# Two softmaxes' results transposed by DMA in five of eight batches, stores of the middle tiles on another queue, and a new order

## The chip, the cores and the metric

The kernel runs on one core of one Trainium2 chip. A core has a matrix engine (TensorE, PE in the profile; its weight loads have a row of their own, PEld), a vector engine (VectorE, DVE), a scalar engine (ScalarE, ACT), GpSimd (POOL) and a queue engine that only issues transfers (SyncE, SP). They run side by side and wait for each other through semaphores; each carries out its own instructions in the order in which the program lists them. The metric is the device time of one execution in microseconds, lower is better.

## What is computed

Attention through 32 packed queries per head, and then a feed-forward block with a squared ReLU, over 8 batches of 576 tokens, 8 heads of 64:

```
def sm_attn(qq, kk, vv):
    s = scale * np.matmul(qq, kk.transpose(0, 1, 3, 2))
    a = exp(s - max(s));  a = a / sum(a)
    return np.matmul(a, vv)
p_packed = sm_attn(p, k, v)                    # first softmax, over 576 keys
out = sm_attn(q, p_packed, p_packed)           # second softmax, over 32 packed keys
x = out.transpose(0, 2, 1, 3).reshape(4608, 512)
g = np.maximum(x @ w_in, 0.0) ** 2             # w_in 512 x 2048
result = g @ w_out                             # w_out 2048 x 512, float32
```

## The kernel before

All matrix work is in bf16, accumulated in float32 in PSUM. The eight heads of a batch are taken as two groups of four (the index `qd`), so that 4 x 32 packed queries fill 128 rows. For each batch b the steps are:

- **Tk, Tq**: VectorE transposes the loaded k and q in 32 x 32 blocks (lines 391 and 396).
- **S1**: scores of the packed queries on TensorE (405, 407), then maximum, exponential and normalization; the normalized result is the tile `e1n` (422).
- **E**: `s1_tr` turns `e1n` by five 128 x 128 transposes on TensorE (428) into PSUM, and `s1_out` copies that to the tile `e1` in SBUF, on VectorE or ScalarE. Once for each `qd`.
- **PV**: `e1` times v (442), and **XT**: the packed values are copied out, in two forms.
- **M**: the packed values times w_in (469), copied out as `M`. The second attention is thus folded into the first feed-forward product: its output is never formed.
- **S2**, **C**: scores of the 576 queries against the packed keys (490, 508), then maximum, difference, exponential, sum and product; the result is `n2` (543).
- **N**: `s2_trh` turns `n2` by four and by five TensorE transposes (552, 554), and `s2_outh` copies them to the tile `a2`, in two halves.
- **F1**: for each of 16 blocks of 128 hidden columns, `f1_mm` multiplies `M` with `a2` over two groups and two halves of 288 tokens (567), `f1_relu` (605) and `f1_sq` (615) make the squared ReLU in `gT`.
- **F2**: for each of the 36 tiles of 128 tokens, 16 matmuls of `gT` with w_out (623); `f2_out` copies the sum to `o_sb` (three buffers) and stores it by four DMAs of 64 KB on SyncE's queue (632).

Batch 0 is handled in smaller halves (`SOLO`). Inputs are loaded by GpSimd's queue (363 to 375), which issues its last load at 91 us of the profile. `keep_clock` puts matmuls on a tile of zeros (306) into TensorE's queue where the plan sees a gap in the first 70 us.

The order of all this is computed when the kernel is built. `Plan` simulates engines, PSUM banks and buffers: a `Step` has pieces with an engine and a cost, the steps it depends on, and a `lag` after its end (for a transfer). Whenever an engine is free, the ready step with the lowest priority value goes next; the priorities are the level of the step's kind plus an entry in `TABLE` that was found by a search. The instructions are then emitted in the order of the plan's starts, and each engine carries out its part in that order, whatever the true durations are.

Of the kernel before, what the change touches and what calls it, by code (L numbers as in the profile page):

```python
# [14 lines left out]
P = 128  # L15
# [34 lines left out]
class Plan:  # L50
# [179 lines left out]
TABLE = {'o': {'F2.10': 9.46, 'Tk.7': 21.4, 'Tq.7': 33.99, 'S1.7': 1.48, 'E.7': 32.14, 'PV.7': 37.91, 'XT.7': 25.64,  # L230
    'M.7': -16.57, 'S2.7': 25.07, 'C.7': 3.76, 'N.7': -24.34, 'F1.7': 11.4, 'F2.6': 17.88, 'M.5': 28.2, 'F2.11': 4.52,
    'P.0': -15.37, 'P.2': 23.02, 'PV.0': 41.78, 'PV.1': -18.07, 'PV.2': -170.61, 'PV.3': 15.6, 'PV.4': 24.74, 'PV.5':
    50.46, 'PV.6': 36.59, 'F2.28': 22.46, 'Tk.2': -5.46, 'Tq.2': 29.94, 'S1.2': -31.94, 'E.2': -12.36, 'XT.2': -89.86,
    'M.2': 21.02, 'S2.2': -17.52, 'C.2': -43.11, 'N.2': -66.16, 'F1.2': -77.2, 'F2.2': 9.33, 'E.1': -3.03, 'S2.0':
    -23.17, 'S2.1': -77.35, 'S2.3': 25.69, 'S2.4': 2.43, 'S2.5': 19.07, 'S2.6': -43.31, 'F1.4': 22.5, 'X.0': 4.02,
    'I2': -4.34, 'Tq.0': 41.62, 'C.3': 12.43, 'I': -21.13, 'Tk.4': 7.8, 'Tq.4': 73.53, 'S1.4': 6.89, 'E.4': -35.44,
    'XT.4': 13.78, 'M.4': 27.57, 'C.4': -22.86, 'N.4': -40.64, 'Tk.3': -2.54, 'Tq.3': 0.13, 'S1.3': -18.78, 'E.3':
    -37.22, 'XT.3': -50.22, 'M.3': 5.0, 'N.3': -11.14, 'F1.3': -41.33, 'F2.7': 8.19, 'Tq.1': -7.08, 'F2.32': -13.57,
    'C.1': -39.73, 'F2.0': 16.2, 'F2.4': 12.03, 'F2.8': -33.24, 'F2.12': -104.27, 'F2.14': -11.93, 'F2.16': -31.57,
    'F2.18': 50.59, 'F2.20': 10.93, 'F2.22': 58.58, 'F2.24': 12.61, 'F2.26': 28.84, 'F2.30': -32.16, 'F2.34': 11.76,  # L240
    'F2.1': 6.19, 'F2.3': 15.65, 'F2.5': -3.27, 'F2.9': 56.43, 'F2.13': 87.78, 'F2.15': 66.49, 'F2.17': 33.58,
    'F2.19': 23.11, 'F2.21': -9.88, 'F2.23': -16.12, 'F2.25': 1.33, 'F2.27': -3.46, 'F2.29': -57.09, 'F2.31': 10.9,
    'F2.33': 10.56, 'F2.35': 8.17, 'FA.0': -13.56, 'XT.1': 1.11, 'E.0': 7.63, 'Tk.6': 27.02, 'Tq.6': 35.38, 'S1.6':
    -0.9, 'E.6': 21.43, 'XT.6': -24.73, 'M.6': -14.77, 'C.6': -27.6, 'N.6': -21.43, 'F1.6': 9.04, 'N.1': -24.39,
    'F1.0': 11.32, 'F1.1': -44.14, 'F1.5': 16.32, 'XT.0': 18.01, 'XT.5': 3.63, 'Tq.5': 37.3, 'Tk.5': 9.59, 'S1.5':
    -29.87, 'E.5': 38.05, 'C.5': 8.51, 'N.5': -3.11, 'X.1': 22.86, 'N.0': -4.85, 'M.0': 35.02, 'M.1': -66.62, 'Tk.1':
    -11.6, 'S1.1': -31.8, 'S1.0': 10.99, 'Tk.0': -5.05}, 'l': {'M.0': -0.4, 'M.1': -0.6, 'M.2': -4.65, 'M.3': -1.76,
    'M.4': 0.35, 'M.5': -0.84, 'M.6': -1.62, 'M.7': 0.92, 'F2.0': -2.74, 'F2.2': -0.16, 'F2.4': 0.92, 'F2.6': -3.13,
    'F2.8': -2.6, 'F2.10': -1.26, 'F2.12': -1.09, 'F2.14': -0.1, 'F2.16': -1.84, 'F2.18': 2.67, 'F2.20': 3.0, 'F2.22':
    -0.29, 'F2.24': 0.61, 'F2.26': 1.34, 'F2.28': -0.04, 'F2.30': -2.69, 'F2.32': 0.95, 'F2.34': 0.34, 'F2.1': -0.07,  # L250
    'F2.3': -1.89, 'F2.5': -1.27, 'F2.7': -2.34, 'F2.9': 2.49, 'F2.11': 4.97, 'F2.13': 0.8, 'F2.15': -0.27, 'F2.17':
    1.19, 'F2.19': 0.34, 'F2.21': -3.12, 'F2.23': -0.33, 'F2.25': 1.96, 'F2.27': 0.05, 'F2.29': 0.52, 'F2.31': -0.53,
    'F2.33': -0.9, 'F2.35': -1.42, 'E.3': 5.1, 'E.5': 0.76, 'N.6': -0.01, 'E.4': 3.71, 'N.7': 0.63, 'E.0': 0.73,
    'XT.1': -0.94, 'XT.3': -0.28, 'XT.4': -5.82, 'XT.5': -0.78, 'X.1': 1.12, 'N.5': -2.41, 'XT.6': -0.27, 'N.0': 1.97,
    'F1.1': -2.19, 'E.6': 0.46, 'E.2': 0.97, 'N.1': 3.16, 'XT.2': -2.27, 'N.3': -0.26, 'N.2': -0.79, 'E.7': 0.19,
    'XT.7': 1.48, 'XT.0': -1.64, 'N.4': -1.73, 'E.1': 1.06, 'X.0': 0.41}, 'w': 0.17, 'm': 33.05}


def kernel_impl(tc, q, k, v, p, w_in, w_out, out):
# [13 lines left out]
    TOKH = (2 * P, S - 2 * P)  # L273

    with ExitStack() as ctx:
# [102 lines left out]
        class Att:  # L378
# [105 lines left out]
            def s2(self, u):  # L484
                self.ps2 = pair(u)
                for tt in range(4):
                    for qd in range(NQD):
                        c0 = (tt % 2) * 2 * P + qd * P
                        for dh in range(2):
                            nc.tensor.matmul(self.ps2[:, tt // 2, c0:c0 + P], lhsT=self.qT[:, qd, dh, tt * P:(tt + 1) * P],  # L490
                                             rhs=self.pq_of(qd, dh), start=(dh == 0), stop=(dh == 1))
# [64 lines left out]

            def s2_outh(self, x, eng):
                self.tile_of("a2", att, [P, NQD, S], BF16)
                cast(eng, self.a2[:, :, x * 2 * P:x * 2 * P + TOKH[x]], self.pst[x].rearrange("p (q n) -> p q n", q=NQD))

        ph, rr = {}, {}

        def f1_mm(a, fb, u):
            ps = ph[a.b, fb] = pair(u)[:, :, :HALF]
            for qd in range(NQD):
                for c in range(2):
                    nc.tensor.matmul(ps[:, c], lhsT=a.M[:, qd, fb * FB:(fb + 1) * FB],  # L567
                                     rhs=a.a2[:, qd, c * HALF:(c + 1) * HALF],
                                     start=(qd == 0), stop=(qd == NQD - 1))

        def new_r(a, fb):
            rr[a.b, fb] = Att.cols(rpool.tile([P, 2 * TOKH[1]], BF16, name="r"))

# [26 lines left out]
        def f1_relu(a, fb, eng, c0=0, c1=2):  # L600
            if c0 == 0:
                new_r(a, fb)
            dst, src = rr[a.b, fb][:, c0:c1], ph[a.b, fb][:, c0:c1]
            if eng is nc.scalar:
                nc.scalar.activation(dst, src, ACT.Relu)  # L605
            else:
                nc.vector.tensor_scalar_max(dst, src, 0.0)

        def f1_sq(a, fb, eng):
            o = (a.b % 2) * S  # L610
            r = rr[a.b, fb]
            if eng is nc.scalar:
                nc.scalar.activation(Att.cols(gT[:, fb, o:o + S]), r, ACT.Square)
            else:
                eng.tensor_tensor(out=Att.cols(gT[:, fb, o:o + S]), in0=r, in1=r, op=ALU.mult)  # L615
# [10 lines left out]
        def f2_out(t, eng):  # L626
            ob = opool.tile([P, NE], F32, name="o_sb")
            cast(eng, ob, po[t])
            for i in range(4):
                b, j = divmod(t * 4 + i, JT)  # L630
                dst = out[b * S:(b + 1) * S, :].rearrange("(a j) e -> j a e", j=JT)[j]
                nc.sync.dma_start(dst, ob[32 * i:32 * i + 32, :])  # L632
# [37 lines left out]
        def tr_steps(b, nm):  # L670
# [6 lines left out]
            return [Step(f"T{nm}.{b}.{qd}", [[[("DVE", 1.36, lambda qd=qd: (T[b].tr_k if nm == "k" else T[b].tr_q)(qd))]]],  # L677
                         [f"L{nm}.{b}.{qd}"] + old + gate(b, 0 if nm == "k" else 2), (), [("kqb", 0, f"L{nm}.{b}.{qd}")]) for qd in QDS]

        def s1_steps(b):  # L680
# [8 lines left out]
            def two(qd):  # L689
                nm = f"E.{b}.{qd}"  # L690
                return Step(nm, [[[("PE", 0.28, lambda: T[b].s1_tr(qd, U[nm]))]],
# [4 lines left out]
        def pv_steps(b):  # L696
            nm = f"PV.{b}.0"
            return [Step(nm, [[[("PE", 0.43, lambda: T[b].pv(0, U[nm]))]]],
                         [f"E.{b}.0", f"Lv.{b}.0", f"Lv.{b}.1", "I2" if b else "I"], banks=AB),
                    Step(f"PV.{b}.1", [[[("PE", 0.43, lambda: T[b].pv(1, U[nm]))]]],  # L700
# [40 lines left out]
        def s2_steps(b):  # L741
# [20 lines left out]
            if b in SOLO:  # L762
# [4 lines left out]
                                                     pre, banks=AB + OB, free=[(2, None)]), nstep(1, [f"S2.{b}.1", f"S2.{b}.2"], AB + OB)]  # L767
            return [Step(nm, [a] + front(3, 1024), pre, banks=HB, free=[(2, None)]),
                    Step(nr, [r] + front(2, 128), pre, banks=AB, free=[(2, None)]),
                    Step(f"C.{b}", chain(4, 1152), [nm, nr])] + [nstep(x, [f"C.{b}"], AB) for x in range(2)]  # L770
# [11 lines left out]
        def f1_steps(b):  # L782
# [3 lines left out]
            for fb in range(NFB):  # L786
                nm = f"F1.{b}.{fb}"
                if b in SPLIT:
                    relu = [[("ACT", 0.42, lambda fb=fb, x=x: f1_relu(T[b], fb, A, x, x + 1)),
                             ("DVE", 0.45, lambda fb=fb, x=x: f1_relu(T[b], fb, V, x, x + 1))] for x in range(2)]  # L790
                else:
                    relu = [[("ACT", 0.66, lambda fb=fb: f1_relu(T[b], fb, A))]
                            + ([("DVE", 0.72, lambda fb=fb: f1_relu(T[b], fb, V))] if b in RELU2 else [])]
                sq = [("DVE", 0.46, lambda fb=fb: f1_sq(T[b], fb, V))]
                if b in SPLIT:
                    sq.append(("ACT", 0.68, lambda fb=fb: f1_sq(T[b], fb, A)))
# [8 lines left out]
        def f2_steps(t):  # L805
# [4 lines left out]
            def deps(fb):  # L810
# [7 lines left out]
        LAG = 2.4  # L818
# [3 lines left out]
        SPLIT = (0,)  # L822
# [12 lines left out]
                        Step("X.0", [NO, [[("DVE", 0.23, lambda h=h: expand_p(0, 2, h, V)),  # L835
                                           ("ACT", 0.3, lambda h=h: expand_p(0, 2, h, A))] for h in range(QH)]], ["P.0"]),
                        Step("P.2", [[[("DVE", 0.97, lambda: tr_p(2, B))]]], ["LP.2"]),
                        Step("X.1", [NO, [[("DVE", 0.5, lambda h=h: expand_p(2, B, h, V)),
                                           ("ACT", 0.8, lambda h=h: expand_p(2, B, h, A))] for h in range(QH)]], ["P.2", "I2"])])
# [75 lines left out]
```

## Time and profile before

| what | value |
|---|---|
| time, median of 3 runs | 264.6 us (264.6, 263.3, 264.8) |
| the profiled execution | 262.87 us, of which 261.0 are the span of the profile |
| busy: PE, DVE, ACT, POOL | 250.4, 196.7, 162.5, 46.3 us (96%, 75%, 62%, 18%) |
| matmuls, weight loads | 2162 each |
| transposes on TensorE, lines 428, 552, 554 | 80 + 64 + 8 |
| F1 matmuls, line 567 | 448, of 288 columns each |
| F2 matmuls, line 623 | 576, of 512 columns each |
| loads by GpSimd's queue | 18.55 MB |
| stores by SyncE's queue | 144 of 64 KB, 1.7 us from issue to landing (median) |

The span is the time from the first to the last record of one profiled execution. Busy time of an engine is the time in which at least one of its instructions runs. Matmuls overlap in the array, so that the duration of one is longer than the time for which it holds the engine: what it costs is the distance from its start to that of the next.

The page also divides the span into 40 slices of 6.5 us, with a digit for the busy tenths of each:

```profile
DVE  5859989989999686997789786965898887535301
ACT  1237877759456868679757498677647754367310
POOL 8645964333423300000000000000000000000000
PEclk9999999999999999999999999999999999999999
DMA  6999999999999996221021110120132102220132
```

POOL works only while it issues loads, and the DMA engines are full for some 105 us and nearly idle afterwards. The granted clock of TensorE (PEclk) is full throughout.

### The profile page before, as it was taken

The numbers are of one execution on the slowest core, as the hardware profiler recorded it, in microseconds if no ns is written. First come the engines' busy times: TensorE is split into PE (matmuls) and PEld (weight loads), VectorE is DVE, ScalarE is ACT, GpSimd is POOL, SyncE is SP. The second block draws the span as 40 slices with busy tenths as digits, with TensorE's granted clock in tenths as the row PEclk, the third lists the DMA queues.
The fourth block names the chain that finished last, engine by engine and source line by source line (L and its number), as shares of the span: only waits on it lengthen the run. The fifth ranks groups of instructions, "written<-read, shape, count | busy, mean of one in ns | idle before, by whom it ended". The sixth has DMA issues, their size and how long they took to land.

```text
span 261.0 us, 5504 instructions
## 1 busy us (share of the span) xinstructions
PE 250.4 (96%) x2162; PEld 145.5 (56%) x2162; DVE 196.7 (75%) x343; ACT 162.5 (62%) x306; POOL 46.3 (18%) x76
## 2 busy tenths in 40 slices
PE   8969999999999999999999999999999999999992
PEld 6656665466554755467564565466535655456440
DVE  5859989989999686997789786965898887535301
ACT  1237877759456868679757498677647754367310
POOL 8645964333423300000000000000000000000000
PEclk9999999999999999999999999999999999999999
DMA  6999999999999996221021110120132102220132
GB/s 108 201 202 208 202 207 199 230 231 227 205 238 229 227 216 117 57 72 37 21 62 44 40 43 0 51 74 0 43 82 51 32 3 60 73 71 0 46 94 64
DMA packets 26426, 28.48 MB, mean 109 GB/s; under 512 B 5408, under 2 KB 17696, under 8 KB 26400
## 3 DMA queue, kind: packets, MB, share of 16 engines
q0 software_dynamic: 18960, 18.55, 43.2%
q1 hardware_dynamic: 6912, 9.45, 13.3%
q8 instruction: 17, 0.28, 0.5%
q10 hardware_dynamic: 528, 0.13, 0.2%
q14 instruction: 9, 0.07, 0.1%
HBM read 37.22 MB, written 9.44 MB: 179 GB/s over the span
## 4 chain that ended last, share of the span: by engine, by line
PE 73%; DMA 13%; POOL 4%; SPq 3%; ACT 3%; issue 1%; DVE 1%; ACTq 0%; POOLq 0%
PE pb L623 40%; PE ps L567 20%; DMA w_in_b<-in_moe_w_in_dram 4%; DMA w_out_b<-in_moe_w_out_dram 4%; DMA q_b<-in_q_dram 3%; SPq L632 3%; PE ps L490 3%; PE ps L405 2%; DMA out_dram<-o_sb 2%; PE pb L442 2%; PE ps L469 2%; ACT r L605 1%; PE pb L428 1%; PE pb L469 1%; POOL pT_bd L336 1%
## 5 line engine op out<-in xcount | busy, mean ns | idle before, releaser
L623 PE MATMUL pb<-w_out_b,gT 128*128 128x512 bf16 x576 | 148.1, 380 | 0.5 <-DMA w_out_b<-in_moe_w_out_dram 0.4
L605 ACT ACTIVATE r<-ps 128x576 bf16<-128x576 f32 x112 | 71.7, 651 | 20.6 <-PE ps L567 15.9
L623 PEld LDWEIGHTS <-gT 128*128 128x128 bf16 x576 | 53.9, 98 | 52.0 <-issue 3.5
L567 PE MATMUL ps<-a,M 128*128 128x288 bf16 x448 | 72.0, 286 | 0.9 <-ACT r L605 0.8
L615 DVE TENSOR_TENSOR gT<-r 128x576 bf16<-128x576 bf16 x112 | 49.9, 455 | 26.8 <-ACT r L605 25.7
L567 PEld LDWEIGHTS <-M 128*128 128x128 bf16 x448 | 43.0, 98 | 24.4 <-issue 3.4
L324 ACT COPY o_sb<-pb 128x512 f32<-128x512 f32 x24 | 14.1, 586 | 27.6 <-PE pb L623 18.9
L396 DVE STREAM_TRANSPOSE kT<-k_b 128x1152 bf16<-128x1152 bf16 x16 | 22.8, 1452 | 1.3 <-DMA k_b<-in_k_dram 1.2
L391 DVE STREAM_TRANSPOSE qT<-q_b 128x1152 bf16<-128x1152 bf16 x16 | 21.6, 1364 | 0.1
L415 ACT ACTIVATE e1x<-ps,n 128x576 bf16<-128x576 f32 x16 | 11.9, 745 | 11.1 <-DVE n L411 11.0
L326 DVE COPY o_sb<-pb 128x512 f32<-128x512 f32 x12 | 8.2, 687 | 12.3 <-DMA out_dram<-o_sb 11.1
L324 ACT CAST M<-ps 128x1024 bf16<-128x1024 f32 (+1 forms) x17 | 14.3, 860 | 3.8 <-PE ps L469 3.8
L306 PEld LDWEIGHTS <-zero 128*128 128x128 bf16 x122 | 12.2, 104 | 6.3 <-issue 2.9
L324 ACT CAST pq_bd<-pb 32x64 bf16<-32x64 f32 x52 | 10.5, 202 | 8.3 <-PE pb L442 7.4
L531 ACT ACTIVATE e<-d 128x1152 bf16<-128x1152 f32 (+2 forms) x10 | 9.7, 969 | 8.6 <-DVE d L525 8.5
L324 ACT CAST M<-pb 128x512 bf16<-128x512 f32 x25 | 13.9, 599 | 1.4 <-PE pb L469 1.3
L368 POOL DMA_DIRECT2D v_b<-in_v_dram x16 | 11.2, 699 | 12.7 <-DMA k_b<-in_k_dram 4.9
L411 DVE TENSOR_REDUCE n<-ps 128x1 f32<-128x576 f32 x16 | 11.8, 744 | 1.9 <-PE ps L407 1.8
L306 PE MATMUL ps<-zero 128*128 128x256 bf16 x79 | 11.2, 301 | 1.3 <-DVE zero L329 1.1
L537 DVE TENSOR_REDUCE t<-e 128x36 f32<-128x1152 bf16 (+2 forms) x10 | 11.0, 1096 | 1.5 <-ACT e L531 1.2
L363 POOL DMA_DIRECT2D k_b<-in_k_dram x16 | 8.7, 542 | 14.1 <-DMA q_b<-in_q_dram 3.7
L363 POOL DMA_DIRECT2D q_b<-in_q_dram x16 | 9.0, 565 | 12.5 <-DMA v_b<-in_v_dram 6.3
(66 smaller groups left out, 236.6 us busy)
## 6 DMA issues: line engine op xcount, KB each, us to landing
out_dram<-o_sb SPq DMA_DIRECT2D x144, 64.0 KB, 1.7
k_b<-in_k_dram POOLq DMA_DIRECT2D x16, 288.0 KB, 12.3
q_b<-in_q_dram POOLq DMA_DIRECT2D x16, 288.0 KB, 12.1
v_b<-in_v_dram POOLq DMA_DIRECT2D x8, 320.0 KB, 12.0
v_b<-in_v_dram POOLq DMA_DIRECT2D x8, 256.0 KB, 11.6
w_in_b<-in_moe_w_in_dram POOLq DMA_DIRECT2D x8, 256.0 KB, 11.2
w_out_b<-in_moe_w_out_dram POOLq DMA_DIRECT2D x8, 256.0 KB, 10.2
p_b<-in_p_dram POOLq DMA_DIRECT2D x1, 192.0 KB, 10.5
```

Of the source, the lines that this page charges most:

```text
L306: nc.tensor.matmul(t, lhsT=zero[:, :P], rhs=zero, start=True, stop=True)
L324: nc.scalar.copy(dst, src)
L363: nc.gpsimd.dma_start(t, src[self.b, qd * QH:(qd + 1) * QH].rearrange("h (a j) d -> (h a) (j d)", j=JT))
L368: nc.gpsimd.dma_start(self.v[64 * i:64 * i + 64, :, :n * D], src[:, :, i * GM * D:(i * GM + n) * D])
L391: nc.vector.transpose(self.qT[:, qd].rearrange("p dh (j a) -> p j dh a", a=32), self.t.q[qd][:].rearrange("p (j dh dl) -> p j dh dl", dh=2 ...
L396: nc.vector.transpose(kT[:, qd].rearrange("p dh (x a j2) -> p j2 x dh a", a=32, j2=2), self.t.k[qd][:].rearrange("p (j2 x dh dl) -> p j2 x ...
L411: nc.vector.tensor_reduce(self.n1[:, qd:qd + 1], self.ps1[qd], axis=AX.X, op=ALU.max, negate=True)
L415: nc.scalar.activation(e1x[:, qd], self.ps1[qd], ACT.Exp, bias=self.n1[:, qd:qd + 1], accum_out=self.d1[:, qd:qd + 1])
L567: nc.tensor.matmul(ps[:, c], lhsT=a.M[:, qd, fb * FB:(fb + 1) * FB], rhs=a.a2[:, qd, c * HALF:(c + 1) * HALF], start=(qd == 0), stop=(qd = ...
L605: nc.scalar.activation(dst, src, ACT.Relu)
L615: eng.tensor_tensor(out=Att.cols(gT[:, fb, o:o + S]), in0=r, in1=r, op=ALU.mult)
L623: nc.tensor.matmul(po[t], lhsT=gT[:, fb, n0:n0 + P], rhs=w_out_b[:, fb, :], start=(fb == 0), stop=(fb == NFB - 1))
```

## The change

For batches 3 to 7 (`BYDMA`):

- `s1_dma` replaces `s1_tr` and `s1_out`: for each `qd`, one transposing DMA of the 512 first columns of `e1n` (four blocks of 128) and one of the last 128, straight into `e1`, on SyncE's queue.
- `s2_dma` replaces `s2_trh` and `s2_outh`: two transposing DMAs of 512 columns into `a2` and one of the 128 columns of the remaining tokens into a new tile `ar`, on SyncE's queue. For this the scores of S2 lie in PSUM with all four token tiles of a group together.
- `f1_mm` therefore multiplies 512 tokens and then 64 tokens, in place of 288 and 288; relu and square then run over 576 neighbouring columns.

The plan gives a first-softmax step 0.5 us on a queue of its own (`SPQ`), a second-softmax step 1.0 us, and both a lag of `DLAG` = 3.5 us. The steps that follow (PV, F1) depend on them as before. For all batches: stores of the output tiles 10 to 27 are issued by GpSimd in place of SyncE; a few step costs are corrected; branches that batch 0 never takes are removed; and `TABLE` has new values, so the order of all steps is another.

```diff
-TABLE = {'o': {'F2.10': 9.46, 'Tk.7': 21.4, ...}, 'l': {...}, 'w': 0.17, 'm': 33.05}
+TABLE = {'o': {'F2.10': 65.17, 'Tk.7': -6.32, ...}, 'l': {...}, 'w': 0.24, 'm': 35.7}
...
+    BYDMA = range(3, B)
...
                 for tt in range(4):
                     for qd in range(NQD):
-                        c0 = (tt % 2) * 2 * P + qd * P
+                        n, c0 = (qd, tt * P) if self.b in BYDMA else (tt // 2, (tt % 2) * 2 * P + qd * P)
...
+            def s2_dma(self):
+                self.tile_of("a2", att, [P, NQD, S], BF16)
+                self.tile_of("ar", small, [P, P], BF16)
+                for qd in range(NQD):
+                    nc.sync.dma_start_transpose(self.a2[:, qd, :4 * P].rearrange("p (t n) -> p t n", n=P),
+                                                self.n2[:, 16 * qd:16 * qd + 16].rearrange("p g i -> p (g i)"))
+                nc.sync.dma_start_transpose(self.ar, self.n2[:, 32:36].rearrange("p g i -> p (g i)"))
+
+            def s1_dma(self, qd):
+                self.tile_of("e1", att, [P, NQD, GM + 1, P], BF16, bufs=1)
+                nc.sync.dma_start_transpose(self.e1[:, qd, :GM], self.e1n[:, qd, :GM * P])
+                nc.sync.dma_start_transpose(self.e1[:, qd, GM], self.e1n[:, qd, S - P:])
...
         def f1_mm(a, fb, u):
+            if a.b in BYDMA:
+                ps = ph[a.b, fb] = pair(u).rearrange("p c n -> p (c n)")[:, :S]
+                for qd in range(NQD):
+                    w = a.M[:, qd, fb * FB:(fb + 1) * FB]
+                    nc.tensor.matmul(ps[:, :4 * P], lhsT=w, rhs=a.a2[:, qd, :4 * P], start=(qd == 0), stop=(qd == NQD - 1))
+                    nc.tensor.matmul(ps[:, 4 * P:], lhsT=w, rhs=a.ar[:, 64 * qd:64 * qd + 64], start=(qd == 0), stop=(qd == NQD - 1))
+                return
...
         def new_r(a, fb):
-            rr[a.b, fb] = Att.cols(rpool.tile([P, 2 * TOKH[1]], BF16, name="r"))
+            r = rpool.tile([P, 2 * TOKH[1]], BF16, name="r")
+            rr[a.b, fb] = r[:, :S] if a.b in BYDMA else Att.cols(r)
...
-                nc.sync.dma_start(dst, ob[32 * i:32 * i + 32, :])
+                (nc.gpsimd if 10 <= t < NT - 8 else nc.sync).dma_start(dst, ob[32 * i:32 * i + 32, :])
...
+                if b in BYDMA:
+                    return Step(nm, [[[("SPQ", 0.5, lambda: T[b].s1_dma(qd))]]], [f"S1.{b}.{qd}"], lag=DLAG)
...
+            if b in BYDMA:
+                last = [Step(f"N.{b}.0", [[[("SPQ", 1.0, lambda: T[b].s2_dma())]]], [f"C.{b}", f1n(b - 2, NFB - 1)], lag=DLAG),
+                        Step(f"N.{b}.1", [[[("-", 0.0, lambda: None)]]], [f"N.{b}.0"])]
+            else:
+                last = [nstep(x, [f"C.{b}"], AB) for x in range(2)]
...
-        LAG = 2.4
+        LAG, DLAG = 2.4, 3.5
```

The corrected costs: a Tk block 1.46 and a Tq block 1.37 in place of 1.36, a PV half 0.40 in place of 0.43, and four costs of expanding p (0.29, 0.42, 0.39 and 0.85 in place of 0.23, 0.3, 0.5 and 0.8).

## The prediction

> **What bounds the kernel now.** I began with the busy time of each engine by stage, cut at 42 us, where the last wait of TensorE (PE) for a weight load ends, and at 255.5 us, where its last matmul starts.
>
> ```profile
> core 0: us, PE busy (x) PEld busy (x) DVE busy (x) ACT busy (x) POOL busy (x), PEclk, DMA share, GB/s
> 0.00:42.00 42.00, 37.78 (x395) 26.01 (x396) 33.55 (x63) 23.31 (x54) 27.98 (x45) 1.00 1.16 189
> 42.00:255.50 213.50, 212.27 (x1767) 119.51 (x1766) 162.41 (x280) 139.21 (x253) 18.34 (x31) 1.00 0.47 95
> 255.50:261.00 5.50, 0.34 (x2) 0.00 (x0) 0.69 (x1) 0.00 (x0) 0.00 (x0) 0.94 0.19 50
> ```
>
> Three stages have three limits. In the first the DMA engines are full and PE's busy time includes 16.55 us of the zero matmuls of line 306 (same view, tile `zero` alone): real work waits for loads. In the second PE is busy for 212.27 of 213.50 us at full granted clock, and DVE (76%) and ACT (65%) are not near full. The last 5.5 us are the last eviction and store. A busy PE could still hide waits, so I read PE's own waits next, all of them:
>
> ```profile
> PE pb L306 <- ACT ppT L324: 2.1, 1, 2.1
> PE ps L306 <- DVE zero L329: 1.1, 1, 1.1
> PE ps L567 <- ACT r L605: 0.8, 3, 0.3
> PE pb L623 <- DMA w_out_b<-in_moe_w_out_dram: 0.4, 1, 0.4
> PE ps L405 <- DVE kT L396: 0.2, 1, 0.2
> PE ps L306 <- ACT M L324: 0.2, 1, 0.2
> ```
>
> Nearly all lie before 42 us; afterwards PE stands about 1 us in all. So from 42 us on the time is PE's amount of work, and a step on PE is worth what it occupies there. The chain of waits agrees: its share by engine begins "PE 73%", and DMA's 13% is in the first stage and the tail.
>
> How long a small matmul occupies PE can't be read from its duration (220 ns for a transpose), because matmuls overlap. The chain gives it; columns are start, length, piece:
>
> ```profile
> 199.12 0.45 PE pb L552 x8
> 199.62 1.08 PE pb L623 x5
> 200.70 0.28 PE pb L428 x5
> 200.98 0.98 PE ps L567 x8
> ```
>
> Eight transposes hold PE 0.45 us and five hold it 0.28: 56 ns each. A 288-column F1 matmul (line 567) holds it 0.98/8 = 122 ns, a 512-column one (623) 216 ns.
>
> **The change part by part.** *TensorE transposes removed.* Per batch the first softmax has 2 x 5, the second 4 + 5: 19. Five batches: 95, times 56 ns = 5.3 us, all after 85 us in this trace, that is in the stage PE fills. Term: -5.3.
>
> The Trainium skill, in "VectorE: DVE Perf Modes", section "The three transpose paths", speaks against this trade: it gives 390 ns for a 128x128 bf16 transpose on TensorE and 1309 ns by DMA, and its rules send such a transpose to TensorE if a PSUM destination will do. The trace differs on the first figure, 56 ns in a stream; by the page's, the removal would be an estimated 95 x 0.39 = 37 us. No run here shows the second.
>
> *Evictions removed.* Twenty copies out of PSUM (10 of `e` at 483 ns on DVE or 692 on ACT, 10 of `a` at 425 to 712): some 11 us on two engines that are not the limit. What hides them is PE's full queue; term 0, and they only shorten chains.
>
> *F1 recut from 288+288 to 512+64 columns*, five batches x 16 x 2 pairs = 160. A 64-column matmul with its own weight load is in the trace, line 407, ahead of a 512-column one:
>
> ```profile
> 189.58 0.22 PE L407 MATMUL ps<-kT,pT_bd 128*128 128x64 bf16 x2
> 189.64 0.38 PE L623 MATMUL pb<-w_out_b,gT 128*128 128x512 bf16 x1
> ```
>
> Two start at 189.58 and the next matmul, with other weights, at 189.64: 30 ns each, so the next load hides behind even this short one. 216 + 30 = 246 against 2 x 122 = 244: 160 x 2 ns = +0.3. Were the 98 ns load exposed, it would be 160 x 0.07 = +11; the row says it isn't. The contiguous relu and square keep their 576 elements: 0.
>
> *35 transposing DMAs on SP's queue*, four and three per batch. None is in the trace, so I bound their delay from the SP stores, which move 64 KB each:
>
> ```profile
> out_dram<-o_sb SPq DMA_DIRECT2D x20, 64.0 KB, 5.1
> out_dram<-o_sb SPq DMA_DIRECT2D x64, 64.0 KB, 1.7
> ```
>
> The first line is 60 to 90 us, under the input loads (DMA share 9 in every slice), the second 105 to 200 us. One issue holds SP 0.42 us. Without loads a half of the first softmax (160 KB, two issues) then takes about 0.42 + 0.42 + 1.7 = 2.5 us, the second softmax (288 KB, three issues) 1.3 + 1.7 = 3.0, or 3.4 if it behaves like the four stores of one tile. Under loads: 0.84 + 5.1 = 5.9. It could be less, as SBUF to SBUF writes no HBM, or more, if transposing is slow. I take 2.5 to 3.5, the unloaded row, because loads are over at 105 us and only batch 3's first softmax (85 us) meets them.
>
> What covers this delay? On PE, PV and F1 wait for it in order, with every F2 matmul behind them. In the trace the time from the last `e1n` product to the second half of PV is 5.7, 7.3, 3.7, 16.7 and 1.8 us (batches 3 to 7: 84.1 to 89.8, 119.5 to 126.8, 133.0 to 136.7, 168.7 to 185.4, 201.7 to 203.5), and from the end of `n2` to the first F1 matmul 4.2, 5.5, 14.7, 4.6, 3.9. The new order is written for 0.5 + 3.5 = 4.0 and 1.0 + 3.5 = 4.5. A delay of 3.5 fits all but the 1.8 by the old order and all by the new. Batch 3 at 5.9 exceeds the new 4.0 by 1.9 and the old 5.7 by 0.2: half-way, +1.0. Without any cover every handover would cost its whole delay, 10 x 3 = 30 us.
>
> SP executes in order: a store that waits for its eviction holds the transposes queued behind it (SP waits long in this trace, up to 44 us, but for its next tile). For tiles 10 to 27 that is just what moves away; tiles 28 on remain beside batch 7's transposes, 1.7 us of issue each, a bound inside the spread above.
>
> *72 stores to GpSimd.* Its issues take 0.53 to 0.72 us here, so 72 x 0.6 = 43 us on an engine idle after 92 us. A tile's store needs 4 x 0.6 + 1.7 = 4.1 us against 3.4; three output buffers cover it, since the densest stretch stores a tile every 4 us (185 to 203 us). If landing went to the 12 us of GpSimd's loads, evictions would wait, as they do at 200.5 us (0.3). Term 0. Freed SP time, 72 x 0.42 = 30 us, is off the path: 0.
>
> *New order table and corrected step costs.* It moves steps on every engine. It can't lower PE's work; below zero it could replace zero matmuls in the first stage, above zero it could open waits. From 16.55 us of filler and 1 us of waits I allow -2 to +2 and take 0.
>
> Sum: -5.3 + 0.3 + 1.0 = -4.0. The profiled execution took 262.87 (span 261.0 and 1.87 around it), so 258.9 for it; it lies 1.7 under the median of 264.6, so **260.5** as a median.
>
> **Rivals.** *First: the handovers give it back.* With delay D at both places, the old covers give waits of 4.5 + 2.3 = 6.8 us at D = 5 and 3.7 + 1.1 = 4.8 at 4.6. For D near 4.8 the saving is gone: about 264, no change. For it: the unknown row, PE's strict order. Against: the unloaded stores.
>
> *Second, slower: transposes go one after the other.* If each 64 KB costs a whole 1.7 us in turn, a first-softmax half needs 4.3 and a second softmax 7.7 us. The F1 handover is the place: old covers give 3.5 + 2.2 + 0 + 3.1 + 3.8 = 12.6 there, 0.6 + 2.5 at PV, so 15.7 - 5.0 = +10.7: 275. It decides over 1% slower from D about 5.2 (7.8 of waits against 5.0 saved). For it: the loaded row of 5.1 shows SP's DMAs can be that late; against: there the loads were in the way, and after 105 us the DMA share is 0.1 to 0.4. The skill's rule is this rival: by 1309 ns a tile, one after the other, nine tiles would take an estimated 11.8 us, worse still; the traces so far neither show nor exclude it.
>
> **How the numbers follow.** Over 1% (2.6 us) is about what a measurement of this kernel tells from no change. Forecast, 256.5 to 262: 0.56, nearly all over 1% faster. First rival, 262 to 267: 0.20. Second, from 267 up to 275: 0.24. A range of 256.5 to 269 leaves out 0.04 below and about 0.16 of the second rival; the forecast's own is 257 to 262.
>
> **What would show it.** Right: PE has 95 matmuls fewer, the stage from 42 us is some 4 to 5 us shorter with PE still over 98% busy; F1 pairs still hold it 0.49 us per four; transposing DMAs land within 4 us; PE's waits for `e1` and `a2` sum to 1 us or so. Wrong: PE waits on DMAs at lines 442 or 567, landing over 5 us, F1's four matmuls nearer 0.6 us, DVE or ACT waiting for `o_sb` in the middle, or more filler at line 306.

## The result, and the profile after

The changed kernel takes 267.56 us (median of 4 runs, 267.07 to 267.93) against 264.5 us before (4 runs): a ratio of 1.0135, 95% interval 1.0101 to 1.0168. A run over 1.5% above the fastest of its kernel is left out of the ratios. The changed kernel is slower by 3.1 us by the medians and some 3.6 by the ratio, where 260.5 us and a gain were forecast. Its profiled execution took 267.56 us, 265.8 of them the span.

The stages, cut as before at 42 us and where the last matmul starts (columns: stretch, its length, then busy time and number of instructions for each engine):

```profile
0.00:42.00 42.00, 35.92 (x374) 25.60 (x378) 30.69 (x59) 22.40 (x52) 27.44 (x44) 1.00 1.15 189
42.00:260.30 218.30, 209.08 (x1665) 106.14 (x1694) 154.17 (x273) 138.66 (x246) 54.29 (x104) 0.99 0.56 107
260.30:265.80 5.50, 0.52 (x3) 0.02 (x1) 0.69 (x1) 0.00 (x0) 0.00 (x0) 0.76 0.22 58
```

The middle stage has grown from 213.5 to 218.3 us, although PE is busy for 3.2 us less in it: PE now stands for 9.2 us there, against 1.2, and the granted clock is no longer full. What PE waits for (view of waits, the longest that are new; columns: us in total, times, longest):

```profile
PE pb L444 <- DMA e<-e1n: 4.8, 6, 2.0
...
PE ps L407 <- DVE kT L398: 1.2, 2, 0.9
...
PE pb L647 <- ACT o_sb L326: 0.9, 2, 0.7
...
PE ps L492 <- DVE gT L639: 0.8, 1, 0.8
...
PE ps L584 <- DMA ar<-n: 0.4, 1, 0.4
```

The first line is PV waiting for the first softmax's transposes. The timeline of PE shows where: 3.7 of the 4.8 us lie at one place, batch 3, and the other 1.1 at batch 6, at 182 us. This is batch 3's part (in brackets the idle time ahead of the piece and what ended it):

```profile
97.81 0.30 PE L444 MATMUL pb<-e,v_b 128*64 128x32 bf16 x8 [0.23 <-DMA e<-e1n]
98.44 0.36 PE L444 MATMUL pb<-e,v_b 128*64 128x32 bf16 x12 [0.33 <-DMA e<-e1n]
100.85 0.30 PE L444 MATMUL pb<-e,v_b 128*64 128x32 bf16 x8 [2.05 <-DMA e<-e1n]
102.22 0.37 PE L444 MATMUL pb<-e,v_b 128*64 128x32 bf16 x12 [1.07 <-DMA e<-e1n]
```

The DMA issues of 88 to 103 us, and then of 105 to 200 us, tell why (size of a plain DMA, then median us from issue to landing):

```profile
out_dram<-o_sb SPq DMA_DIRECT2D x8, 64.0 KB, 8.0
...
e<-e1n SPq DMA_TRANSPOSE x4, 10.0
```

```profile
e<-e1n SPq DMA_TRANSPOSE x12, 3.0
a<-n SPq DMA_TRANSPOSE x8, 3.1
ar<-n SPq DMA_TRANSPOSE x4, 2.9
```

Batch 3's four land 9.1 to 10.3 us after their issue, while the input loads still fill the DMA engines; all others have a median near 3. SyncE's queue and the chain of waits give the times (start, length; the last line is the landing of the fourth):

```profile
87.98 1.28 SPq L569 DMA_TRANSPOSE e<-e1n  x1
89.32 1.22 SPq L570 DMA_TRANSPOSE e<-e1n  x1
90.64 1.21 SPq L569 DMA_TRANSPOSE e<-e1n  x1
91.89 1.23 SPq L570 DMA_TRANSPOSE e<-e1n  x1
...
91.89 10.29 DMA e<-e1n
```

The two halves of batch 3's `e1n` are ready at 85.21 and 87.24 us (ends of line 424 on VectorE). So it takes 13.2 and 14.9 us from there until the second DMA of a half has landed. The standing PE then loses its clock. By stage (the seventh value after the length is the granted clock):

```profile
97.00:103.00 6.00, 2.25 (x44) 1.36 (x44) 3.13 (x3) 1.14 (x4) 0.00 (x0) 0.98 1.27 206
103.00:106.20 3.20, 3.06 (x12) 1.41 (x12) 0.58 (x1) 1.52 (x8) 0.00 (x0) 0.50 0.52 146
```

In 97 to 103 us PE works 2.25 of 6 us, and the next 3.2 us run at half the clock, another 1.6 us lost. The Trainium skill, "TensorE: Matmul & The Clock Gate", Part 1, tells of such a gate: half clock after an idle window of about 3.4 us, full again after a busy one. The trace agrees on the length: the half clock lasts 3.41 us. But PE wasn't idle for all of such a window here: the longest single wait is 2.05 us, and in the 3.41 us ahead of the half clock PE works 0.84.

A second reading of PE's stage leaves durations aside. I count PE's weight loads by line and multiply by what each kind of matmul holds PE for (216 ns for 512 columns, 122 for 288, 56 for 128, 29 for 64, 21 for a PV and 35 for an M matmul; zero matmuls count nothing). What is left of a stretch is time without useful work:

```
us of the span   work before  after   without work: before  after
0 to 42                20.3    18.9          21.7     23.1
42 to 85               41.4    39.9           1.6      3.1
85 to 125              38.7    32.9           1.3      7.1
125 to 175             48.7    48.8           1.3      1.2
175 to 200             24.6    22.4           0.4      2.6
200 to the end         54.3    59.8           6.7      6.0
whole span            227.9   222.7          33.1     43.1
```

The work fell by 5.2 us (this follows from the number of matmuls of each kind, since both columns use the same prices) and the rest grew by 10.0. Most of that, 5.8 us, lies around batch 3; 1.5 us at 42 to 85 us, ahead of any transposing DMA, and 2.2 us at 175 to 200 us.

### The profile page after: what moved, and what is told of

Read it like the earlier page. It is cut to its first block, busy times and chain, and to the rows that moved or that the text cites. A ratio compares the mean times of both kernels' runs of the same rounds, so it can differ in the third digit from the quotient of the medians.

```text
span 265.8 us, 5340 instructions
## 1 busy us (share of the span) xinstructions
PE 245.5 (92%) x2039; PEld 131.8 (50%) x2072; DVE 185.6 (70%) x332; ACT 161.1 (61%) x297; POOL 81.7 (31%) x148
## 4 chain that ended last, share of the span: by engine, by line
PE 60%; DMA 20%; DVE 5%; SPq 4%; ACT 3%; POOL 3%; issue 3%; DVEq 0%; ACTq 0%; POOLq 0%
PE pb L647 33%; PE ps L583 11%; DMA e<-e1n 7%; PE ps L589 4%; DMA w_in_b<-in_moe_w_in_dram 4%; DMA q_b<-in_q_dram 4%; DMA w_out_b<-in_moe_w_out_dram 3%; PE ps L492 2%; PE ps L584 2%; DMA out_dram<-o_sb 2%; PE ps L407 2%; PE ps L471 2%; PE pb L444 1%; SPq L656 1%; SPq L563 1%
## 5 line engine op out<-in xcount | busy, mean ns | idle before, releaser
L647 PE MATMUL pb<-w_out_b,gT 128*128 128x512 bf16 x552 | 143.1, 381 | 3.2 <-ACT o_sb L326 0.9
L647 PEld LDWEIGHTS <-gT 128*128 128x128 bf16 x576 | 52.7, 98 | 60.0 <-issue 6.4
L639 DVE TENSOR_TENSOR gT<-r 128x576 bf16<-128x576 bf16 x112 | 48.9, 452 | 28.1 <-ACT r L627 27.5
L656 POOL DMA_DIRECT2D out_dram<-o_sb x72 | 35.4, 499 | 103.5 <-ACT o_sb L326 55.6
L583 PE MATMUL ps<-a,M 128*128 128x512 bf16 x153 | 47.5, 380 | 0.2
L584 PE MATMUL ps<-ar,M 128*128 128x64 bf16 x160 | 30.8, 193 | 0.8 <-DMA ar<-n 0.4
L326 ACT CAST M<-ps 128x1024 bf16<-128x1024 f32 (+1 forms) x20 | 17.4, 885 | 10.1 <-PE ps L471 10.1
L589 PE MATMUL ps<-a,M 128*128 128x288 bf16 x128 | 20.7, 286 | 0.1
L326 ACT CAST pq_bd<-pb 32x64 bf16<-32x64 f32 x44 | 8.9, 203 | 10.1 <-PE pb L444 7.2
L326 ACT CAST M<-pb 128x512 bf16<-128x512 f32 x26 | 14.6, 597 | 0.0
## 6 DMA issues: line engine op xcount, KB each, us to landing
w_out_b<-in_moe_w_out_dram POOLq DMA_DIRECT2D x8, 256.0 KB, 10.3
```

What stands on the lines that cost most here:

```text
L326: nc.scalar.copy(dst, src)
L583: nc.tensor.matmul(ps[:, :4 * P], lhsT=w, rhs=a.a2[:, qd, :4 * P], start=(qd == 0), stop=(qd == NQD - 1))
L584: nc.tensor.matmul(ps[:, 4 * P:], lhsT=w, rhs=a.ar[:, 64 * qd:64 * qd + 64], start=(qd == 0), stop=(qd == NQD - 1))
L639: eng.tensor_tensor(out=g, in0=r, in1=r, op=ALU.mult)
L647: nc.tensor.matmul(po[t], lhsT=gT[:, fb, n0:n0 + P], rhs=w_out_b[:, fb, :], start=(fb == 0), stop=(fb == NFB - 1))
L656: (nc.gpsimd if 10 <= t < NT - 8 else nc.sync).dma_start(dst, ob[32 * i:32 * i + 32, :])
```

## The experiments

Theory A: batch 3's first-softmax transposes land late under the loads, and PE stands for them. Theory B: the new order is the loss, wherever its waits appear. Theory C: GpSimd's stores hold up the transposes or the evictions. Ratios are to the kernel before, run on the same chip (263.1 to 263.6 us there).

**Batch 3's PV on a constant.**

```diff
-rhs=self.e1[:, qd, g, h * NP:(h + 1) * NP]
+rhs=(ident[:, h * NP:(h + 1) * NP] if self.b == 3 else self.e1[:, qd, g, h * NP:(h + 1) * NP])
```

> The changed kernel with one operand exchanged: the PV matmuls of batch 3 read columns of the identity tile in place of e1, so they wait for no transposing DMA; all DMAs still run and every engine keeps its order (batch 3's packed values are therefore not the reference's). Theory A (the transposes of batch 3's first softmax, issued under the input loads, land after 9.4 to 10.2 us and PE stands for them): the 5.5 us of PE idle between 95 and 105 us, the half clock that follows it included, go, and the time falls by 4.5 to 6 us to about 262 to 263. Theory B (the loss is the new order's, spread over the span): the wait moves to the next dependent step and the time stays within 1.5 us of 267.5.

261.04 us, ratio 0.9905 (0.9873 to 0.9937), 2.3 points below the changed kernel or 6.1 us (6.5 by the medians, a little more than A's 4.5 to 6). The transposing DMAs themselves are as late as before, up to 10.0 us; only PE no longer waits for them. The same stretch, now:

```profile
97.00:103.00 6.00, 6.00 (x83) 3.61 (x80) 5.84 (x8) 3.26 (x12) 0.00 (x0) 1.00 1.22 221
103.00:106.20 3.20, 3.20 (x17) 1.47 (x15) 3.16 (x7) 1.97 (x3) 0.92 (x2) 1.00 0.52 134
```

PE is busy throughout at full clock, and the time does not come back later. One handover cost more than the whole loss. A holds, B as the main cause falls.

**No handover waits at all.**

```diff
+rhs=(ident[...] if self.b in BYDMA else self.e1[...])
-rhs=a.a2[:, qd, :4 * P]
+rhs=w_out_b[:, qd, :4 * P]
-rhs=a.ar[:, 64 * qd:64 * qd + 64]
+rhs=w_out_b[:, 2, 64 * qd:64 * qd + 64]
```

> The changed kernel in which neither PV nor F1 of batches 3 to 7 waits for a transposing DMA: PV reads the identity tile in place of e1, F1 reads w_out in place of a2 and ar (so these batches' results are not the reference's); all DMAs still run, every engine keeps its order. It shows what all ten handovers together cost. Theory A (batch 3's first softmax alone is nearly all of it): at most 2 us below the kernel with only batch 3's PV on a constant (261.0), so 259 to 261. Rival (the other nine handovers cost as much again): 255 to 258.

258.96 us, ratio 0.9837 (0.9795 to 0.9879). This is the lower edge of A's range. The other nine handovers cost 0.7 points, about 1.8 us; the intervals of the two runs overlap a little, so that this size is rough. What is left is a gain of 1.6% or 4.3 us (3.2 to 5.4), with every transposing DMA still issued: close to the 5.0 us that PE's work should have given.

**Stores back on SyncE**, all other instructions in the same order.

```diff
-(nc.gpsimd if 10 <= t < NT - 8 else nc.sync).dma_start(dst, ob[32 * i:32 * i + 32, :])
+nc.sync.dma_start(dst, ob[32 * i:32 * i + 32, :])
```

> The changed kernel with the stores of tiles 10 to 27 back on SyncE; every other instruction in the same order. Theory A: GpSimd's stores cost nothing, so the time stays or rises by 0 to 2 us (from 267.5), since transposes of batches 4 to 7 queue behind stores that wait for evictions. Theory C (GpSimd's stores, issued while transposes are in flight, delay these, as at 176 us where one takes 5.2 us): the wait of 1.3 us before batch 6's PV goes and the time falls by 1 to 3 us.

279.21 us, ratio 1.0589 (1.0553 to 1.0626): neither theory had the size. C falls, and A's 0 to 2 us is 12. SyncE's queue in this run, around batch 5's first softmax, whose second half of `e1n` is ready at 151.58 us:

```profile
145.96 2.53 SPq L563 DMA_TRANSPOSE a<-n  x2
148.53 1.23 SPq L565 DMA_TRANSPOSE ar<-n  x1
149.86 1.95 SPq L656 DMA_DIRECT2D out_dram<-o_sb  x4
151.91 1.20 SPq L569 DMA_TRANSPOSE e<-e1n  x1
153.16 1.23 SPq L570 DMA_TRANSPOSE e<-e1n  x1
154.49 2.89 SPq L656 DMA_DIRECT2D out_dram<-o_sb  x4
157.47 1.20 SPq L569 DMA_TRANSPOSE e<-e1n  x1
```

The queue is never empty: the transposes of that half start 5.9 us after their data, behind the stores of a tile and the half before. What holds them in this piece is mostly the time that SyncE needs to issue what stands ahead, not a store waiting for its eviction. PE's waits at PV grow to

```profile
PE pb L444 <- DMA e<-e1n: 11.2, 10, 2.1
```

and the granted clock falls to half at three places in the middle instead of one.

**The stores alone**, in the kernel before.

```diff
-nc.sync.dma_start(dst, ob[32 * i:32 * i + 32, :])
+(nc.gpsimd if 10 <= t < NT - 8 else nc.sync).dma_start(dst, ob[32 * i:32 * i + 32, :])
```

> The kernel before with nothing changed but the stores of tiles 10 to 27 on GpSimd, all engines' order the same. If these stores cost nothing by themselves: within 0.5% of before (263.5 here). If their slower issue (0.50 against 0.42 us each) and landing (2.0 against 1.7) hold up evictions through the three output buffers: 1 to 3 us more.

263.59 us, ratio 1.0001 (0.9978 to 1.0025). By itself the move is worth nothing; beside the transposes it is worth 12 us.

**Transposing DMAs from batch 4 on.**

```diff
-BYDMA = range(3, B)
+BYDMA = range(4, B)
```

> The changed kernel with TensorE transposes kept for batch 3 too (DMA transposes for 4 to 7 only); the plan is made anew from batch 3's first softmax on, with the same table. Theory A: the 5.5 us at 95 to 105 us go, 19 transposes come back (1.1 us): about 263, no granted clock of one half in the middle. Theory B: 266 to 269.

262.2 us (10 runs), ratio 0.995 (0.9928 to 0.9973): faster than both kernels, no half clock in the middle. A again. PE's work is 223.7 us, 4.1 below before, and 1.3 us of that arrives.

**Without the loads of batches 5 to 7.**

```diff
+if self.b >= 5:      # in dma_kq
+    nc.gpsimd.memset(t, 0.0)
+    return
...
+if self.b >= 5:      # in dma_v
+    return
```

> The changed kernel without the loads of k, q and v for batches 5 to 7 (k and q are set to zero by GpSimd, v of an earlier batch is used, so these batches' results are not the reference's); every engine keeps its order. The loads then end well before 88 us. Theory A (contention: batch 3's transposes land late because the DMA engines are full of loads): their landing falls from 9.4 to 10.2 us to 2.5 to 4 us, PE's waits at PV of batch 3 and the half clock go, time 260.5 to 263. Rival (they are late for a reason of their own, or because of the stores behind them on SyncE): landing stays above 8 us and the time above 266.

The transposes of batch 3 land as expected (DMA issues of 91 to 100 us):

```profile
e<-e1n SPq DMA_TRANSPOSE x4, 2.3
```

and PE's stand at 95 to 105 us falls from 5.5 to 0.1 us: the loads are what made them late, since the stores on SyncE's queue are still there. The time misses its expectation, 264.2 to 269.5 us in four runs, and there is no ratio. A new wait came at 67 us, ahead of the place in question:

```profile
PE pb L435 <- DVE e1n L429: 2.4, 1, 2.4
```

with half clock for 6.8 us behind it. There the one VectorE instruction that makes `e1n` takes 3.70 us in place of 0.37, while GpSimd runs the added memsets from 63.1 to 69.2 us; that these hold it up is likely, but not tried by itself. So this run tells the landing, not the time.

**The delay told to the plan.**

```diff
-lag=DLAG)
+lag=DLAG + (8.0 if b == 3 else 0.0))
```

> The changed kernel with the plan told that batch 3's first-softmax transposes take 8 us longer (lag 11.5 in place of 3.5); the order is made anew from there with the same table. Theory A: PE gets other work for that time, the wait of batch 3 goes: 261 to 264, no half clock in the middle. Rival (the work behind batch 3 has no such slack, or an order that the table was not fitted to loses as much): 265 to 270, with new waits after 110 us.

277.68 us (272.8 to 278.7), ratio 1.0419 (1.0323 to 1.0514); a miss, above both ranges. Its profile is of one of the longer runs (276.8 us of span), so only the places count: the order made anew waits for transposes again, 7.0 us in all and up to 1.9 at once, and the clock falls three times. The next run but one tests whether the short lags were the reason.

**Measured costs, batches 4 to 7**, on the kernel of `range(4, B)`.

```diff
-("SPQ", 0.5, lambda: T[b].s1_dma(qd))
+("SPQ", 2.5, lambda: T[b].s1_dma(qd))
-("SPQ", 1.0, lambda: T[b].s2_dma())
+("SPQ", 3.75, lambda: T[b].s2_dma())
-LAG, DLAG = 2.4, 3.5
+LAG, DLAG = 2.4, 2.5
```

> DMA transposes for batches 4 to 7, with the measured costs in the plan: 2.5 us of SyncE for a first-softmax half, 3.75 for the second softmax, lag 2.5, in place of 0.5, 1.0 and 3.5. If the idle time of PE that is left after 125 us (2.1 us at 125 to 150, 2.2 at 175 to 200 with the old costs) comes from these too small costs: 259 to 261.5. If the table, found with the old costs, matters more: 262 to 270.

262.33 us (10 runs), ratio 0.9944 (0.9924 to 0.9964): no wait of PE for a transposing DMA is left, and no time is gained over the run before with batches 4 to 7; it is the second of the two ranges that holds. The stand at 125 to 150 us goes (2.1 to 0.6 us) and that at 175 to 200 stays (2.6): there PE waits for VectorE and ScalarE.

**Measured costs for batches 3 to 7**, with 10 us of lag for batch 3's first softmax (the edit above, and `+ (7.5 if b == 3 else 0.0)`).

> DMA transposes for batches 3 to 7 with the measured costs in the plan (2.5 and 3.75 us of SyncE, lag 2.5, and 10 for batch 3's first softmax); same table, order made anew from batch 3 on. If the 277.7 us of the run with only batch 3's lag corrected came from the too short lags of the other batches, whose waits summed to 7 us and brought the clock down twice more: 262 to 266 and no PE wait for a transposing DMA over 0.5 us. If an order other than the one the table was fitted to is the loss: above 268.

269.63 us, ratio 1.0243 (1.0197 to 1.0288). The waits of the later batches are gone, as expected, so the short lags were some 5 us, by the ratios, of the run with only batch 3's lag. But PE still waits 1.5 us at once for a transposing DMA before 125 us, where at most 0.5 was expected, and 7.0 us of PE time without work stand at 115 to 125 us, with half clock from 118.5 to 128.8: batch 3's own steps now come so late that PE runs out of work that doesn't need them. Planning for the late landing did not save it, with this table.

**The old order with the transposes.**

```diff
-TABLE = {'o': {'F2.10': 65.17, ...
+TABLE = {'o': {'F2.10': 9.46, ...
```

> The changed kernel with the table and the step costs of before (transposes by DMA for batches 3 to 7, stores on GpSimd). Up to 85 us the order is that of before. Theory A: the first 85 us lose the 3.0 us of extra PE idle that the new order has there (23.2 against 26.2), but batch 3's transposes still land under the loads after about 10 us and PE stands: 264 to 268. Theory B: the new order is all of the loss, so 258 to 261.

287.24 us, ratio 1.0883 (1.0829 to 1.0938): both theories' ranges are missed, A's 264 to 268 by some 20 us and B's 258 to 261 by more. The waits of PE for transposes sum to 17.6 us:

```profile
PE pb L443 <- DMA e<-e1n: 8.7, 5, 3.2
PE ps L582 <- DMA a<-n: 5.0, 2, 3.0
PE ps L583 <- DMA ar<-n: 3.9, 3, 2.3
```

At 65 to 85 us it has 0.2 us without work against 1.9 in the changed kernel, as A expected; A's error is that all handovers, not batch 3's alone, wait in this order. With batches 4 to 7 and the measured costs:

> Table and step costs of before, DMA transposes for batches 4 to 7 with the measured costs in the plan, stores on GpSimd. It separates the two halves of the 287 us of the old order. If these were the delays that the plan did not know: 258 to 264, with at most 0.5 us idle at 65 to 85 us. If the old table is simply a bad order once the steps are others: above 266, with PE waiting for other engines and not for DMAs.

267.06 us, ratio 1.0147 (1.009 to 1.0205): the second of the two expectations, a bad order for these steps, holds. Both halves are there: some 19 of the 23 us go with batch 3 and with the delays that the plan did not know (two changes at once, which this run does not tell apart), and what remains are mostly waits for ScalarE and VectorE.

**The new order without transposing DMAs** (`BYDMA = range(B, B)`).

> The changed kernel with TensorE transposes for all batches: the new table and step costs, stores of tiles 10 to 27 on GpSimd, no transposing DMA. Up to 85 us the order is that of the changed kernel, from there it is planned anew. If the new order has a cost of its own: the 1.5 us of extra PE idle at 65 to 85 us stay, PE's work is that of before, and the time is 265 to 268 (before: 263.6). If it has none: 262.5 to 264.5.

269.82 us, ratio 1.0252 (1.0219 to 1.0285), somewhat above the range. The 1.7 us at 65 to 85 us are there, and nearly 5 at 150 to 200. So a table goes with its steps. With transposes on TensorE throughout, the new table, with its step costs, is 2.5% worse than the old one; with DMA for batches 4 to 7 and the measured costs, it is 2.0 points better (0.9944 against 1.0147). Taken to quite other steps, either is 1.5 to 2.5% worse than the kernel before. So what an order is worth can't be told apart from its steps by such exchanges; only the runs that keep the order (the constants, the stores) price a single wait.

## Why the prediction was wrong

- *PE is the bound, -5.3 us for 95 transposes, +0.3 for the recut F1.* Right. The matmuls counted in the trace are those forecast; F1's pairs start every 0.24 to 0.25 us in the chain (0.246 forecast), and without handover waits 4.3 us arrive. The evictions' 0 has no run of its own.
- *Batch 3 at +1.0 us.* This term failed: it measures 6.1 us. The bound was built from a store of 64 KB under loads (5.1 us), two issues of 0.42 and half of an excess over the cover. In the run each of the four transposing DMAs holds SyncE 1.2 us and lands after some 10 us, and SyncE first stands 2.3 us, which the profile puts down to the landing of a store. The delay from the product to the landing, 13.2 and 14.9 us, is over twice the forecast 5.9. The cover was larger than forecast too: PE comes to PV at 97.6 us, 10.3 us after the second half's product, where 4.0 to 5.7 were taken; without that the stand would have been longer. That a stand of PE also costs clock (1.6 of the 6.1) was not in it at all.
- *Other handovers at 0, delay 2.5 to 3.5 us.* Mis-sized: 1.8 us. Without loads a first-softmax half takes 1.25 + 2.4 to 3.0 = 3.7 to 4.3 us and the second softmax 2.5 + 2.9 = 5.4, since an issue costs 1.2 and not 0.42 us. The new order's covers take most of it. The dearest of these places is batch 6, with waits of 1.1 us.
- *GpSimd's stores at 0, and the freed SP time "is off the path: 0".* Right for the stores alone (1.0001), wrong for the queue that they leave to the transposes: without the move the changed kernel is 12 us slower. The queue bound stood in the prediction ("a store that waits for its eviction holds the transposes queued behind it") and got no price.
- *The new order at -2 to +2.* Inside its range: from 1.0135, 2.3 points are batch 3 and 0.7 the other handovers; the remaining -1.6% is 0.7 us short of the forecast -5.0 us, less than the interval allows for. Waits at 76 and 184 us (0.9 and 0.8 us, for an eviction on ScalarE and for VectorE) fit an order that costs a little, but no run prices it alone. In all, -5.0 + 6.1 + 1.8 + 0.7 = +3.6 us, against the forecast -4.0.
- *The rivals.* The first rival's mechanism won, handovers with strict order on PE, but mainly at one place and with a delay of 13 to 15 us, not at ten places with 5. The second, transposes one after the other at a fixed price per 64 KB, is not what happened: SyncE does issue them one after the other, but 128 columns and 512 columns hold it for the same 1.2 us, and unloaded landing is 3 us for either. That the time lies in the second rival's band, and inside the stated 256.5 to 269, is luck.
- *The rule against the trade.* The Trainium skill, "VectorE: DVE Perf Modes", section "Rules for kernel authors", sends a 128x128 transpose to TensorE where a destination in PSUM will do. The runs agree for batch 3: with its transposes on TensorE the kernel is 1.85 points faster than the changed one. They do not for the later batches: the kernel with DMA from batch 4 on, its order and stores included, is 0.5% faster than before. There a landing of 3 us lies beside PE's work, and TensorE's 56 ns do not. The Trainium skill's 1309 ns for a DMA transpose ("VectorE: DVE Perf Modes", section "The three transpose paths") does not fit as a price for each tile in turn: a DMA of four tiles lands within 0.2 us of one of a single tile (3.1 and 2.9 us).

The chance of 0.56 for a gain rested on "loads are over at 105 us and only batch 3's first softmax (85 us) meets them". That was true; the one batch was enough.

## What to carry to other kernels

Before moving a step from a full engine to DMA, price its latency in the stage in which it will run, not in the mean: ask of every single handover what else fills the DMA engines then, and leave those on the engine that lie under the loads. Free an in-order queue that gets such transfers of other traffic: here moving the stores cost nothing by itself (1.0001) and was worth 12 us beside the transposes, more than the step moved. A wait on the bounding engine costs more than its length if the engine's clock falls behind it: here 3.7 us of waits cost 6.1.

## What the runs showed of the hardware that was not expected

- A transposing DMA holds its queue's engine for a median of 1.22 us (512 columns of the first softmax) and 1.24 us (128 columns): four times the data for the same hold. A store of 64 KB holds it for 0.42.
- Under loads the transposes land after 10.0 us against 3.0 without. The stores of 64 KB suffer alike: from 1.7 to 5.1 us in the kernel before, and to 8.0 for the eight of the changed kernel that SyncE issues right behind batch 3's transposes. The trace has the transposes as packets of 256 bytes, 1280 for batch 3's four DMAs, at a median of 31 ns each under loads and 18 without; the stores go in packets of 2 KB. That the many small packets each wait their turn beside the loads' larger ones would fit, but it was not tried by itself, and the stores' lateness speaks against packet size as the whole cause.
- Waits of PE of 3.7 us in all within 5 us, none longer than 2.05, are followed by 3.41 us at half clock.
